# Loading q and k in 512-byte runs, with the tokens of each 128-block kept even-then-odd through masks, V and output

## The chip, the cores and the metric

The kernel runs on one core of one Trainium2 chip. The metric is the device time of one execution in microseconds (us). The profile's span is about 2 us shorter than that time, because it goes from the first to the last instruction. In the profile's lines PE is TensorE (PEld its weight loads), DVE VectorE, ACT ScalarE, POOL GpSimd and SP SyncE; the granted clock is the share of its full clock that TensorE was given.

## The reference

It is an attention layer followed by a two-branch dense layer. Half of the heads see all earlier tokens, the others only the first 4 tokens and a window of 64.

```python
B, H, S, D = 4, 8, 768, 64          # q, k, v: float32
scores = q @ k.T / sqrt(D)          # causal; for "streaming" heads also: sink of 4 or window of 64
a   = softmax(scores)
x   = (a @ v), heads side by side   # 3072 tokens x 512
out = maximum(x @ w1, x @ w2) @ w_out    # 512 -> 1024 -> 512, float32 out
```

The inputs q and k are drawn with a standard deviation of 0.1, so all scores are small and the softmax is nearly flat. The comparison with the reference does not notice when the tokens of q or k are permuted, but it does notice a wrong order of v.

## The kernel before

The 32 heads are worked on in 16 pairs. Each pair's q, k and v come in by DMA as float32, GpSimd casts them to bfloat16, and q and k are transposed so that the head dimension lies on the partitions. For the first four pairs TensorE does the transposing and VectorE or ScalarE evacuates; from the fifth pair on (`FIRST_QK_DMA = 4`) a DMA transpose does it. Scores, exponentials, masks, the product with v and the dense layer follow. A small planner in the program fixes the order on every engine when the kernel is built, with a cost for each operation; nearly all DMAs are issued by SyncE, in one program order.

```python
# one load of a pair; only the first pairs' q and k come as 512-byte runs (two tokens side by side)
wide = which < 2 and i < FIRST_QK_DMA
pat = ("h (m p r) d -> p h m (r d)", dict(p=128, r=2)) if wide else ("h (n p) d -> p h n d", dict(p=128))
...
    nc.sync.dma_start(out=dst, in_=src.rearrange(pat[0], **pat[1]))
ld_ops[tag, i] = P.add({"DMA": 1.15 if wide else 1.75}, fn, ...)

# transposing q or k, from the fifth pair on: one DMA of 128 x 768
nc.sync.dma_start_transpose(
    out=P[tt, i].rearrange("p (n c) -> p n c", c=128),
    in_=P[tb, i].rearrange("p n h d -> p (n h d)"))

# the first four pairs: evacuation of TensorE's transposes puts two-token runs back in order
if i < FIRST_QK_DMA:
    o = o.rearrange("q (m p r) -> q m r p", p=128, r=2)
    in_ = in_.rearrange("q (m r p) -> q m r p", p=128, r=2)
ev(eng)(out=o, in_=in_)

# scores of one step: (k block j, first q column, columns, offset in the PSUM bank)
for (j, q0, w, off) in segs:
    for hh in range(2):
        nc.tensor.matmul(P["sc", i, st, hh][:, off:off + w],
            lhsT=kt[64 * hh:64 * hh + 64, j * 128:(j + 1) * 128],
            rhs=qt[64 * hh:64 * hh + 64, q0:q0 + w], start=True, stop=True, ...)
...
# store of 128 output rows
nc.sync.dma_start(out=out[r0:r0 + 128, :], in_=P["ot", b, g, t])
```

The softmax here doesn't subtract the row's maximum and nothing guards it: scores larger than these inputs give would overflow.

Of the kernel before, what the change touches and what calls it, by code (L numbers as in the profile page):

```python
# [133 lines left out]
def kernel(  # L134
# [81 lines left out]
    def constants():  # L216
# [5 lines left out]
        col = consts.tile([128, 256], F32)  # L222
        nc.vector.memset(col[:, 0:1], 0.0)
        w = 1
        while w < 256:
            nc.vector.tensor_scalar_add(out=col[:, w:2 * w], in0=col[:, 0:w], scalar1=float(w))
            w *= 2
        rowt = consts.tile([128, 32], F32)
        nc.vector.transpose(rowt, col[:, 0:32])
        row = consts.tile([128, 1], F32)  # L230
        for qd in range(4):
            nc.vector.tensor_scalar_add(
                out=row[32 * qd:32 * qd + 32, :], in0=rowt[32 * qd:32 * qd + 32, 0:1],
                scalar1=float(32 * qd))
        nc.vector.tensor_scalar(out=ident, in0=col[:, 0:128], scalar1=row, scalar2=None, op0=ALU.is_equal)
# [23 lines left out]
    def near(j):  # L259
        return (j, 128 * j, min(256, S - 128 * j), 256 * (j % 2))  # L260

    STEPS = (
        ("near", [near(0), near(1)]),
        ("far0", [(0, 256, 512, 0)]),
        ("near", [near(2), near(3)]),
        ("far", [(1, 384, 384, 0), (3, 640, 128, 384)]),
        ("near", [near(4), near(5)]),
        ("far", [(2, 512, 256, 0)]),
    )
    NS = len(STEPS)  # L270
# [4 lines left out]
    def plan_load(i, b, hp, which):  # L275
        src = (q, k, v)[which][b, 2 * hp:2 * hp + 2]
        tag = ("ldq", "ldk", "ldv")[which]
        wide = which < 2 and i < FIRST_QK_DMA
        pat = ("h (m p r) d -> p h m (r d)", dict(p=128, r=2)) if wide else ("h (n p) d -> p h n d", dict(p=128))

        def fn(eng):
            dst = P[tag, i]
            if which < 2 and not wide:
                dst = dst.rearrange("p h m (r d) -> p h (m r) d", d=D)
            nc.sync.dma_start(out=dst, in_=src.rearrange(pat[0], **pat[1]))  # L285
        ld_ops[tag, i] = P.add({"DMA": 1.15 if wide else 1.75}, fn, acq=[(tag, (tag, i))], prio=(len(ld_ops),))
# [14 lines left out]
    def plan_pair(i, b, hp):  # L301
# [15 lines left out]
        for which in range(2):  # L317
            tb, tt = (("qb", "qt"), ("kb", "kt"))[which]

            if i >= FIRST_QK_DMA:  # L320
                def move(eng, tb=tb, tt=tt):
                    nc.sync.dma_start_transpose(
                        out=P[tt, i].rearrange("p (n c) -> p n c", c=128),
                        in_=P[tb, i].rearrange("p n h d -> p (n h d)"))
                tops.append(P.add({"DMA": 0.9}, move, deps=[casts[which]], acq=[(tt, (tt, i))], rel=[(tb, i)],
                                  prio=(0, i, which)))
                continue
# [7 lines left out]
            def evac(eng, which=which, tt=tt):  # L335
                o, in_ = P[tt, i], P["mmT", i, which].bitcast(BF16)[:, 0:S]
                if i < FIRST_QK_DMA:
                    o = o.rearrange("q (m p r) -> q m r p", p=128, r=2)
                    in_ = in_.rearrange("q (m r p) -> q m r p", p=128, r=2)
                ev(eng)(out=o, in_=in_)  # L340
            t = P.add({"PE": 0.34}, tr, deps=[casts[which], ident_op], acq=[("mm", ("mmT", i, which)), (tt, (tt, i))],
                      rel=[(tb, i)], prio=(1, i, which))
            tops.append(P.add({"DVE": 0.56, "ACT": 0.72} if i >= FIRST_QK_DMA else {"DVE": 1.02, "ACT": 1.02}, evac, deps=[t],
# [4 lines left out]
        def qk(st):  # L348
            kind, segs = STEPS[st]
            n = segs[-1][3] + segs[-1][2]  # L350

            def fn(eng):
                qt, kt = P["qt", i], P["kt", i]
                for (j, q0, w, off) in segs:
                    for hh in range(2):
                        nc.tensor.matmul(  # L356
                            P["sc", i, st, hh][:, off:off + w],
                            lhsT=kt[64 * hh:64 * hh + 64, j * 128:(j + 1) * 128],
                            rhs=qt[64 * hh:64 * hh + 64, q0:q0 + w],
                            start=True, stop=True, skip_group_check=True)  # L360
            return fn, n, kind, segs
# [46 lines left out]
        for st in range(NS):  # L408
            kind, segs = STEPS[st]

            def fn(eng, st=st, segs=segs):
                for hh in range(2):
                    at, po, vb = P["at", i, st, hh], P["po", i, hh], P["vb", i]
                    for si, (j, q0, w, off) in enumerate(segs):
                        for t in range(w // 128):
                            qb_ = q0 // 128 + t
                            nc.tensor.matmul(
                                po[:, qb_ * (D + 1):(qb_ + 1) * (D + 1)],
                                lhsT=at[:, off + t * 128:off + (t + 1) * 128],
                                rhs=vb[:, hh, j, :],  # L420
                                start=(st == 0 and si == 0 and t == 0),
                                stop=(st == NS - 1 and si == len(segs) - 1 and t == w // 128 - 1),
                                skip_group_check=True)
            nblk = sum(s[2] for s in segs) // 128
# [79 lines left out]
    def plan_dense(b):  # L504
        mm = "mm" if b < B - 1 else "sc"
        prev = [None]
        for g in range(NG):
# [24 lines left out]
            for t in range(GT // 128):  # L532
# [22 lines left out]
                def store(eng, g=g, t=t, c0=c0):  # L555
                    r0 = b * S + c0
                    nc.sync.dma_start(out=out[r0:r0 + 128, :], in_=P["ot", b, g, t])
# [74 lines left out]
```

## Time and profile before

| | kernel before |
|---|---|
| time, median of 2 runs | 212.63 us (211.14 to 214.13) |
| span of the profiled run, granted clock | 208.5 us, 0.992 |
| first scores of the fifth pair start at | 49.2 us |
| first scores of the last pair start at | 148.6 us |
| last score matmul | 155.8 us |

I call the time up to 49.2 us the first stage, the 99.4 us from there to the first scores of the last pair the middle, and the 52.8 us behind the last score matmul the tail. These starts are counted in the trace by the number of score matmuls of a pair, which is the same for all pairs (20 before, 36 after).

From the page of the kernel before, the DMA packets, and the chain that ended last by engine:

```profile
DMA packets 98916, 37.84 MB, mean 181 GB/s; under 512 B 87632, under 2 KB 93776, under 8 KB 98896
PE 42%; DMA 26%; DVE 13%; SPq 6%; ACT 5%; issue 3%; POOL 2%; POOLq 0%; ACTq 0%; DVEq 0%
```

Nine packets in ten are under 512 bytes; these are what the change goes for. In this trace a packet of 256 bytes takes 18 ns in the median, one of 512 bytes 29 ns.

SyncE's own work is easy to pass over, since issuing is not counted as busy in the page's first part. The timeline of SyncE in the kernel before, cut from the middle; the columns are start, duration in us, engine, line, operation and tiles:

```profile
114.04 1.31 SPq L322 DMA_TRANSPOSE qt_97<-qb_90  x1
115.82 1.21 SPq L322 DMA_TRANSPOSE kt_99<-kb_92  x1
117.13 0.53 SPq L557 DMA_DIRECT2D out_dram<-ot_125  x1
117.71 0.42 SPq L285 DMA_DIRECT2D qn_82<-in_q_dram  x1
118.19 0.83 SPq L285 DMA_DIRECT2D kn_85<-in_k_dram  x1
```

A transpose takes SyncE 1.2 to 1.3 us, a store 0.53, loads 0.4 to 0.8. Between them are gaps of up to half a microsecond. Adding up all its issues in the middle gives 78.7 of 99.4 us: 28 transposes 41.7, 20 loads of q and k 15.6, 10 of v 11.7, 11 stores 9.7.

### The profile page before, as it was taken

How to read it: one execution, taken by the hardware profiler on the slowest of the kernel's cores; microseconds unless marked ns; L12 is line 12 of the kernel's file. 1: busy time of each engine (PE TensorE's matmuls, PEld its weight loads, DVE VectorE, ACT ScalarE, POOL GpSimd, SP SyncE). 2: the span in 40 equal slices, each digit the busy share in tenths (PEclk: the TensorE clock that was granted, in tenths of full speed). 3: DMA queues.
4: the chain of work that ended last, by engine and by line, in shares of the span. 5: the costliest groups of instructions: out<-in, count | busy, mean ns of one | idle time of the engine just before them, and what ended most of it. 6: DMA issues, size and time to landing. Idle time of an engine off the chain costs nothing.

```text
span 208.5 us, 4406 instructions
## 1 busy us (share of the span) xinstructions
PE 183.5 (88%) x1702; PEld 95.2 (46%) x1702; DVE 119.5 (57%) x273; ACT 124.0 (59%) x240; POOL 47.6 (23%) x59
## 2 busy tenths in 40 slices
PE   0388886999999799959997999979999999999992
PEld 0244553544554356523463545534454465444540
DVE  7799989957796477614574357427454084030700
ACT  2489699724888788947866795959692200212021
POOL 0155547053333132331231332314000000000000
PEclk9999999999999999988999999999999999999999
DMA  4999999969999999999999999999630210212112
GB/s 117 268 344 323 258 350 410 250 129 220 236 174 240 176 246 218 173 195 191 233 175 207 229 251 205 228 171 252 156 27 15 89 50 0 101 53 101 50 50 101
DMA packets 98916, 37.84 MB, mean 181 GB/s; under 512 B 87632, under 2 KB 93776, under 8 KB 98896
## 3 DMA queue, kind: packets, MB, share of 16 engines
q1 hardware_dynamic: 98752, 37.56, 87.1%
q8 instruction: 13, 0.21, 0.5%
q14 instruction: 7, 0.06, 0.1%
q10 hardware_dynamic: 144, 0.01, 0.0%
HBM read 25.17 MB, written 6.29 MB: 151 GB/s over the span
## 4 chain that ended last, share of the span: by engine, by line
PE 42%; DMA 26%; DVE 13%; SPq 6%; ACT 5%; issue 3%; POOL 2%; POOLq 0%; ACTq 0%; DVEq 0%
PE bank_80 L543 8%; DMA vn_87<-in_v_dram 6%; DMA kn_86<-in_k_dram 6%; SPq L285 4%; PE bank_79 L543 4%; PE bank_79 L514 4%; DMA kt_100<-kb_93 3%; PE bank_80 L514 3%; DMA kn_84<-in_k_dram 3%; DMA vn_89<-in_v_dram 3%; PE bank_80 L495 3%; DMA out_dram<-ot_125 3%; PE bank_74 L543 2%; PE bank_73 L543 2%; DMA kn_85<-in_k_dram 2%
## 5 line engine op out<-in xcount | busy, mean ns | idle before, releaser
L514 PEld LDWEIGHTS <-wd_bf 128*128 128x128 bf16 x256 | 23.0, 98 | 16.6 <-issue 3.0
L368 ACT ACTIVATE at_101<-bank_73 128x512 bf16<-128x512 f32 x16 | 9.6, 597 | 12.4 <-PE bank_74 L356 12.4
L379 DVE TENSOR_TENSOR at_101<-at_101,msk 128x512 bf16<-128x512 bf16 x16 | 8.0, 500 | 12.0 <-ACT at_101 L368 12.0
L356 PE MATMUL bank_73<-qt_98,kt_100 64*128 64x256 bf16 (+1 forms) x48 | 9.2, 271 | 5.9 <-DMA kt_100<-kb_93 5.9
L356 PEld LDWEIGHTS <-kt_100 64*128 64x128 bf16 x160 | 5.6, 94 | 17.1 <-issue 8.5
L543 PEld LDWEIGHTS <-gt_124 128*128 128x128 bf16 x96 | 8.9, 100 | 9.9 <-issue 1.4
L543 PEld LDWEIGHTS <-gt_123 128*128 128x128 bf16 x96 | 8.6, 98 | 9.8 <-issue 0.8
L379 DVE TENSOR_TENSOR at_109<-at_109,msk 128x384 bf16<-128x384 bf16 x16 | 7.9, 493 | 8.9 <-ACT at_109 L368 8.8
L368 ACT ACTIVATE at_107<-bank_75,bias_j 128x512 bf16<-128x512 f32 x16 | 11.1, 695 | 2.4 <-PE bank_76 L356 2.3
L356 PEld LDWEIGHTS <-kt_99 64*128 64x128 bf16 x160 | 5.5, 95 | 13.2 <-issue 8.7
L368 ACT ACTIVATE at_103<-bank_75,bias_64 128x512 bf16<-128x512 f32 x16 | 11.1, 692 | 0.6 <-PE bank_76 L356 0.6
L356 PE MATMUL bank_73<-qt_97,kt_99 64*128 64x256 bf16 (+1 forms) x48 | 9.5, 276 | 2.2 <-DVE kt_99 L340 1.1
L527 DVE TENSOR_SCALAR gt_124<-bank_80 128x384 bf16<-128x384 f32 x9 | 5.0, 558 | 10.8 <-ACT ot_127 L553 5.8
L368 ACT ACTIVATE at_104<-bank_76,bias_64 128x512 bf16<-128x512 f32 x16 | 11.1, 696 | 0.0
L368 ACT ACTIVATE at_108<-bank_76,bias_j 128x512 bf16<-128x512 f32 x16 | 11.1, 691 | 0.0
L368 ACT ACTIVATE at_111<-bank_75,bias_j 128x256 bf16<-128x256 f32 x16 | 7.7, 480 | 5.2 <-PE bank_76 L356 5.2
L368 ACT ACTIVATE at_105<-bank_73 128x512 bf16<-128x512 f32 x16 | 9.8, 613 | 1.6 <-PE bank_74 L356 1.6
L543 PE MATMUL bank_79<-wo_bf,gt_124 128*128 128x512 bf16 x40 | 10.1, 379 | 0.0
L553 ACT COPY ot_125<-bank_80 128x512 f32<-128x512 f32 x3 | 1.8, 585 | 14.0 <-PE bank_80 L543 14.0
L379 DVE TENSOR_TENSOR at_105<-at_105,msk 128x512 bf16<-128x512 bf16 x16 | 8.0, 502 | 3.6 <-ACT at_105 L368 3.6
L543 PE MATMUL bank_80<-wo_bf,gt_123 128*128 128x512 bf16 x40 | 10.0, 380 | 0.0
L368 ACT ACTIVATE at_106<-bank_74 128x512 bf16<-128x512 f32 x16 | 9.9, 621 | 0.0
(225 smaller groups left out, 494.8 us busy)
## 6 DMA issues: line engine op xcount, KB each, us to landing
w_f<-in_moe_w_dram SPq DMA_DIRECT2D x4, 1024.0 KB, 9.2
qn_81<-in_q_dram SPq DMA_DIRECT2D x6, 384.0 KB, 4.7
kn_84<-in_k_dram SPq DMA_DIRECT2D x6, 384.0 KB, 5.6
vn_87<-in_v_dram SPq DMA_DIRECT2D x6, 384.0 KB, 6.5
wo_f<-in_moe_w_out_dram SPq DMA_DIRECT2D x2, 1024.0 KB, 8.2
out_dram<-ot_125 SPq DMA_DIRECT2D x8, 256.0 KB, 2.3
out_dram<-ot_126 SPq DMA_DIRECT2D x8, 256.0 KB, 2.4
out_dram<-ot_127 SPq DMA_DIRECT2D x8, 256.0 KB, 2.4
```

Of the source, the lines that this page charges most:

```text
L285: nc.sync.dma_start(out=dst, in_=src.rearrange(pat[0], **pat[1]))
L356: nc.tensor.matmul(P["sc", i, st, hh][:, off:off + w], lhsT=kt[64 * hh:64 * hh + 64, j * 128:(j + 1) * 128], rhs=qt[64 * hh:64 * hh + 64, ...
L368: nc.scalar.activation(out=P["at", i, st, hh][:, 0:n], in_=P["sc", i, st, hh][:, 0:n], func=ACT.Exp, scale=scale, bias=bias)
L379: nc.vector.tensor_mul(out=at[:, 0:n], in0=at[:, 0:n], in1=mk)
L495: nc.tensor.matmul(P["mmM", c], lhsT=w2t[:, f, c * 128:(c + 1) * 128], rhs=wo_bf[:, f, :], start=(f == 0), stop=(f == FC - 1))
L514: nc.tensor.matmul(P["mmH", b, g, f][:, 0:GT], lhsT=wd_bf[:, c, f * 128:(f + 1) * 128], rhs=P["xt", b][:, c, g * GT:(g + 1) * GT], start=( ...
L527: nc.vector.tensor_relu(out=o, in_=i_)
L543: nc.tensor.matmul(ps, lhsT=lhsT, rhs=rhs, start=(i == 0), stop=(i == KC + FC - 1))
L553: ev(eng)(out=P["ot", b, g, t], in_=P["mmY", b, g, t])
```

## The change

The intent: all q and k are to be loaded as runs of 512 bytes (two neighbouring tokens), not only the first four pairs'. That leaves the even tokens of a block apart from the odd ones after the transpose. Instead of sorting them back, the kernel keeps each 128-token block even-then-odd everywhere: masks, rows of v, rows of the output. To get that order, each DMA transpose, load of v and store is split into two of 64 partitions. The even blocks are laid ahead of the odd ones, so that one half-transpose fills one contiguous half of the transposed tile.

```diff
-        wide = which < 2 and i < FIRST_QK_DMA
...
-            nc.sync.dma_start(out=dst, in_=src.rearrange(pat[0], **pat[1]))
-        ld_ops[tag, i] = P.add({"DMA": 1.15 if wide else 1.75}, ...)
+            if which < 2:
+                nc.sync.dma_start(out=dst, in_=src.rearrange("h (m p r) d -> p h m (r d)", p=128, r=2))
+            else:
+                by_r = src.rearrange("h (n p r) d -> r p h n d", p=64, r=2)
+                for r in range(2):
+                    nc.sync.dma_start(out=dst[64 * r:64 * r + 64], in_=by_r[r])
+        ld_ops[tag, i] = P.add({"DMA": 1.2 if which < 2 else 1.85}, ...)
...
-                    nc.sync.dma_start_transpose(
-                        out=P[tt, i].rearrange("p (n c) -> p n c", c=128),
-                        in_=P[tb, i].rearrange("p n h d -> p (n h d)"))
+                    for half in range(2):
+                        nc.sync.dma_start_transpose(
+                            out=P[tt, i][:, half * 384:half * 384 + 384].rearrange("p (n c) -> p n c", c=64),
+                            in_=P[tb, i][64 * half:64 * half + 64].rearrange("p n h d -> p (n h d)"))
...
-                    nc.sync.dma_start(out=out[r0:r0 + 128, :], in_=P["ot", b, g, t])
+                    rows = out[r0:r0 + 128, :].rearrange("(p r) f -> r p f", r=2)
+                    for r in range(2):
+                        nc.sync.dma_start(out=rows[r], in_=P["ot", b, g, t][64 * r:64 * r + 64, :])
... (cut: position constants and masks in the new order; evacuation of TensorE's transposes in
     runs of 64; score matmuls by runs of blocks, 576 in place of 320; v's block of each tile)
```

## The prediction

> **What bounds the kernel now.** I read the page's slices first, then busy time by stretch, then the chain of waits in each stretch, then the DMA landings and single lines. The slices show no engine that is full from end to end. VectorE is nearly full in the first quarter, the DMA engines until about 150 us, TensorE from there on:
>
> ```profile
> PE   0388886999999799959997999979999999999992
> DVE  7799989957796477614574357427454084030700
> DMA  4999999969999999999999999999630210212112
> ```
>
> So I cut the span where the kind of work changes. The columns are the busy time of each engine, the granted clock, the DMA share and GB/s:
>
> ```profile
> 10.00:42.00 32.00, 26.95 (x340) 15.99 (x341) 30.42 (x59) 27.23 (x53) 15.36 (x16) 1.00 1.12 321
> 49.00:149.00 100.00, 92.96 (x974) 46.42 (x972) 57.26 (x135) 76.82 (x154) 27.81 (x33) 0.98 1.22 210
> 156.00:208.50 52.50, 48.52 (x270) 24.61 (x268) 15.96 (x31) 8.10 (x15) 0.00 (x0) 1.00 0.16 61
> ```
>
> From 10 to 42 us VectorE (the third busy time) works 30.4 of 32 us and the chain lies on it. From 49 us (first scores from DMA-transposed k) to 149 us (scores of the last pair) the DMA share is over 1 while only 210 GB/s move. After 156 us DMA and the others rest, and TensorE runs the dense matmuls that are left. The chain inside the middle stretch, its longest pieces:
>
> ```profile
> 62.08 4.18 DMA kn_85<-in_k_dram
> 69.17 6.94 DMA kn_86<-in_k_dram
> 79.73 7.22 DMA vn_87<-in_v_dram
> 90.59 5.29 DMA out_dram<-ot_125
> 99.52 6.08 DMA vn_89<-in_v_dram
> 128.28 5.53 DMA kn_86<-in_k_dram
> 138.56 6.05 DMA vn_87<-in_v_dram
> ```
>
> These are loads of q, k, v that stand behind one another in one queue, so this stretch goes at the pace of that queue. TensorE looks 93% busy there, but that counts pipeline time: summing its matmuls at their start-to-start spacings (216 ns for 512 columns, 163 ns for 384, 30 ns for the 65-column ones) gives only some 78 us of work in the 100. TensorE can take a faster supply, but not a much faster one. The median times from issue to landing in the middle stretch, and the two lines that the change touches most:
>
> ```profile
> qn_81<-in_q_dram SPq DMA_DIRECT2D x4, 384.0 KB, 4.5
> vn_88<-in_v_dram SPq DMA_DIRECT2D x3, 384.0 KB, 6.7
> L322 SPq DMA_TRANSPOSE kt_99<-kb_92 x6: 1209/1212/2598, 45.0 to 134.9; - x6
> L340 DVE COPY kt_100<-bank_80 x2: 1019/1021/1023, 14.2 to 29.7; 128x768 bf16<-128x768 bf16 x2
> ```
>
> From the landings I take what each transfer costs the queue when it is full (the distance between one landing and the next): a load in 256-byte runs 1.75 us; a transpose 0.66 us (two issued at 93.95 and 95.26 land at 98.62 and 99.27); an output store about 0.95 us. A load in 512-byte runs, as the first four pairs use them, is 1.38 us apart (18.68, 20.05, 21.43).
>
> [...] the packet records have 18 ns for a 256-byte packet and 29 ns for one of 512 (medians), 14 against 18 bytes per ns. [...] No transfer of the kernel before takes half of the partitions[...]; the changed kernel has 128 of them (32 of v, 48 transposes, 48 stores). [...] the 128-column PE transposes start 55 to 56 ns apart.
>
> **The change part by part.**
>
> *First stage, on VectorE.* The evacuation of the PE transposes now writes runs of 64 elements instead of every second one. It takes 1.02 us, eight times (six on VectorE); the plain copy of the same 128x768 (xt_120) takes 0.54. That is 6 x 0.47 = 2.8 us off VectorE if the new pattern copies as the plain one. Against it: six more small constant instructions (about 0.15 us each, +0.9), partly in a gap of 1.04 us that VectorE has at 8.2 us; and the built order moves two weight casts (0.6 us each) from GpSimd to VectorE. Net: 1 to 2 us earlier, I take **-1.5**.
>
> *Middle stage, on the queue.* From 49 to 149 us about 29 loads land (19 of q and k, 10 of v), with 22 transposes of q and k, 6 of x, and 14 stores. Before: 29 x 1.75 + 28 x 0.66 + 14 x 0.95 = 50.8 + 18.5 + 13.3 = 83 us of the 100; the rest are stalls, such as those around 70, 96, 108 and 136 us, where the packets of a transpose are held for 0.6 to 2 us. The change saves 19 x (1.75 - 1.38) = **-7.0 us**. It pays for this with halves:
> - v in two DMAs of 64 partitions. Now 393 KB in 1.75 us is 225 GB/s. [...] 10 x 0.15 = +1.5.
> - stores in two of 64 rows. Now 262 KB in 0.95 us is 276 GB/s; [...] +2.5.
> - transposes in two of 64 partitions. Now 197 KB in 0.66 us is 298 GB/s; [...] +2.
>
> SyncE's issue is a second price. A transpose takes it 1.21 us at least, a load 0.42, a store 0.33. If the time of a transpose goes with its size, two halves cost little more; if not, SyncE's 28 transposes of the middle stage become 50. The least it has to do in 100 us is 51 us now (28 x 1.21 + 29 x 0.42 + 14 x 0.33) and 61 to 86 after, still below the limit, but the latency of each k would grow by up to 1.2 us. I add +1 for this. Middle stage in sum: -7.0 + 1.5 + 2.5 + 2 + 1 = **0**, with a spread of some 6 us to each side.
>
> *TensorE.* The near blocks are no longer neighbours, so the score matmuls go from 320 to 576: 256-column pieces become two of 128. A pair of heads runs side by side: the 64x256 ones start in pairs every 105 ns, so two 128-column pairs at 56 ns each add 7 ns, some 128 times: +0.9 us spread over the span, mostly in the middle's slack.
>
> *Last stage.* The order on each engine is fixed at build time by a planner that was told of faster loads. In the built order the up-projection matmuls behind the last score matmul go from 100 to 128, the down-projections stay at 144. So 28 x 0.160 = **+4.5 us** of dense work leaves the middle for a tail in which TensorE is full. In return the middle carries 4.5 us less; since that stage is only about 78% full of matmuls, I count -2.5 of it. The last store is two DMAs, the second issued 0.33 us later: +0.4.
>
> *Sum:* -1.5 + 0 + 0.5 + 4.5 - 2.5 + 0.4 = about **+1.4 us** from 210.3 in the profiled run. The two timed runs scatter from 211.1 to 214.1, and I shade the middle estimate down[...]: **212.5 us**, as good as no change.
>
> **The rivals.** *A: the queue gains and the halves are free.* For it: landings follow one another without a gap, so the halves may merge in the queue. Then the middle is 7 us shorter, the first stage 1.5, and the moved 4.5 us cost at most 2.5: about 206. *B: the halves cost more than the runs save*[...] by SyncE. For it: transposes already hold packets for up to 2 us, and half of the long chain pieces are not q or k. Then the middle is 6 us longer and the moved work comes on top: 219 or 220. *C: TensorE takes over.* Speeding up the loads only moves the wait to TensorE's fixed order, and the moved tail shows in full: 210 to 214. This is nearest to my sum.
>
> **Range and chances.** From A to B: 206 to 220. A and B seem about equally likely to me, and C likelier than either; faster by over 2% (below 208.4) 0.26, within 2% 0.50, slower 0.24.
>
> **What the profile after would show.** Right: q and k landings 1.4 us apart, packets under 512 B fewer by some 37,000 (24 loads of 1,536); evacuations of the first pairs at 0.55 to 0.6 us; [...] packets of the stores longer than the present 85 ns even in the quiet tail[...]; the stretch behind the last score matmul longer by 4 to 5 us. Wrong: a middle stretch under 95 us (halves free) or over 104 us (halves dear); half-transposes that take SyncE 1.2 us each; or a middle in which TensorE waits for its own order and not for k.

## More of the kernel before

In the chain, "SPq" is the time in which SyncE's issuing of DMAs was what everything waited for: 6% here.

## The result

The changed kernel took **241.38 us** (median of 2 runs, 240.19 to 242.56) against 212.63: it is slower, by a ratio of 1.135 (95% interval 1.093 to 1.177). A ratio here is the mean time of one kernel's fast runs over that of the other's fast runs of the same rounds, so it is not quite the ratio of the medians quoted. Executions over 1.5% slower than the fastest of the same kernel are left out of the means. The prediction of 212.5, and its range up to 220, missed.

| us | before | after | difference | predicted |
|---|---|---|---|---|
| first stage | 49.2 | 53.1 | +3.9 | -1.5 |
| middle, first scores of pair 5 to those of pair 16 | 99.4 | 120.2 | +20.8 | about 0, less 2.5 |
| tail, behind the last score matmul | 52.8 | 58.2 | +5.4 | +4.9 |
| span | 208.5 | 238.4 | +29.9 | |

The rest of the span, the last pair's own scores, is about 7 us in both. The page of the changed kernel, its slices and packets, then its chain by engine:

```profile
PE   0498986999869789979297929896999999999992
DVE  7668788864442654644154604384455308210700
DMA  5999999969998887988685989696853031053313
DMA packets 81896, 37.89 MB, mean 159 GB/s; under 512 B 52176, under 2 KB 76752, under 8 KB 81872
PE 41%; DMA 32%; SPq 15%; POOL 4%; issue 2%; ACT 1%; DVE 1%; POOLq 0%; ACTq 0%
```

The rows for DMA and TensorE, nearly unbroken nines before, now have sevens and eights in the middle: neither is full. The packets went down as intended, those under 512 bytes by 35,456. And SPq went from 6% to 15% of the chain. Busy time in stretches cut by the same rule as before:

```profile
10.00:42.00 32.00, 26.16 (x372) 18.68 (x374) 24.37 (x54) 25.39 (x50) 14.02 (x14) 0.95 1.10 305
53.00:173.00 120.00, 97.07 (x1088) 50.05 (x1100) 54.17 (x128) 77.58 (x151) 28.06 (x33) 0.90 0.90 170
180.00:238.30 58.30, 53.35 (x302) 27.50 (x302) 18.21 (x35) 10.96 (x21) 0.00 (x0) 0.98 0.27 59
```

In the middle line the DMA share is 0.90 (it was 1.22), the rate 170 GB/s (210), VectorE and ScalarE do about the same work in 20 us more, and the granted TensorE clock is 0.90 (0.98). So every engine in that line is less loaded than before, and something else sets the pace. In the first line VectorE works 24.4 of 32 us (30.4): by this count it no longer fills the first stage. The third is the tail, which I cut at 180 us now. SyncE's timeline in the same part of the pipeline:

```profile
134.23 4.07 SPq L345 DMA_TRANSPOSE qt_97<-qb_90  x2
138.39 2.51 SPq L345 DMA_TRANSPOSE kt_99<-kb_92  x2
140.96 0.59 SPq L303 DMA_DIRECT2D qn_83<-in_q_dram  x1
141.65 1.23 SPq L479 DMA_TRANSPOSE xt_122<-x_118  x1
142.97 1.18 SPq L583 DMA_DIRECT2D out_dram<-ot_125  x2
144.20 0.59 SPq L303 DMA_DIRECT2D kn_86<-in_k_dram  x1
144.83 1.36 SPq L307 DMA_DIRECT2D vn_89<-in_v_dram  x2
146.30 1.62 SPq L345 DMA_TRANSPOSE qt_98<-qb_91  x1
```

Each line starts within about 0.1 us of the end of the one before: in this stretch SyncE has no pause. "x2" with 2.51 us is the two halves of one k. The sum over the middle is 111.4 of 120.2 us (93%; 79% before): 50 transposes 70.4, 20 loads of q and k 15.6, 20 halves of v 14.1, 18 halves of stores 11.3. The lines of two transposes of the changed kernel, minimum, median and maximum in ns:

```profile
L345 SPq DMA_TRANSPOSE qt_97<-qb_90 x12: 1197/1260/2202, 45.8 to 159.5; - x12
L345 SPq DMA_TRANSPOSE kt_99<-kb_92 x12: 1186/1250/2664, 49.2 to 162.1; - x12
```

A transpose of 64 partitions takes SyncE 1.19 us at least here, one of 128 took 1.21. **Halving the data did not halve the issue.**

The queue shows the other side. I measured the distance from one landing to the next where a transfer was issued at least 1 us before the one ahead of it landed, so that it had to stand in line (medians):

| in the queue, us | before | after |
|---|---|---|
| load of q or k | 1.81 | 1.42 |
| load of v | 2.39 | 2 x 1.11 |
| transpose of q or k | 0.70 | 2 x 0.40 |
| store of 128 rows | 0.85 | 2 x 0.36 |

For the queue the change is a gain: the loads of q and k give 20 x 0.39 = -7.8 us, the halved transposes cost 22 x 0.1 = +2.2. The row of v can't be read as a gain: its ten values before go from 1.6 to 3.3 us, their median is 2.39 or 2.06 as one counts the loads issued in the middle or those landed there, and a whole v took 1.75 us in a_all_whole and 1.73 in a_whole_v_store (experiments below). Against these, two halves cost 0.4 to 0.5 us more. A whole store took 0.69 and 0.68 us there, so its halves (0.72) cost about nothing. In sum the queue gains some 2 to 6 us. But only 26 of 44 half-transposes of q and k found such a line at all (17 of 21 before). The median from issue to landing of a k says it too:

```profile
kt_99<-kb_92 SPq DMA_TRANSPOSE x6, 4.2
kt_99<-kb_92 SPq DMA_TRANSPOSE x12, 2.5
```

It fell from 4.2 us to 2.5: the halves find a shorter line. More often than before, the queue waits for SyncE.

One more prediction held. The evacuations of the first pairs' transposes, 1.02 us before, in the changed kernel on VectorE and ScalarE:

```profile
L360 DVE COPY kt_100<-bank_80 x2: 557/558/558, 15.0 to 31.7; 128x768 bf16<-128x768 bf16 x2
L360 ACT COPY qt_97<-bank_79 x1: 792/792/792, 8.5 to 8.5; 128x768 bf16<-128x768 bf16 x1
```

### The profile page after: what moved, and what is told of

Same layout as the page of the kernel before. It is cut to its first block, busy times and chain, and to the rows that moved or that the text cites.

```text
span 238.4 us, 5062 instructions
## 1 busy us (share of the span) xinstructions
PE 195.6 (82%) x1938; PEld 106.3 (45%) x1958; DVE 116.1 (49%) x279; ACT 127.5 (53%) x243; POOL 46.2 (19%) x57
## 4 chain that ended last, share of the span: by engine, by line
PE 41%; DMA 32%; SPq 15%; POOL 4%; issue 2%; ACT 1%; DVE 1%; POOLq 0%; ACTq 0%
PE bank_79 L567 7%; PE bank_80 L567 7%; SPq L345 6%; DMA qn_82<-in_q_dram 5%; SPq L307 5%; DMA kt_99<-kb_92 4%; DMA kn_84<-in_k_dram 4%; DMA vn_88<-in_v_dram 4%; DMA wo_f<-in_moe_w_out_dram 3%; PE bank_79 L538 3%; DMA kn_86<-in_k_dram 3%; PE bank_77 L441 3%; PE bank_73 L380 3%; PE bank_80 L538 2%; DMA qn_83<-in_q_dram 2%
## 5 line engine op out<-in xcount | busy, mean ns | idle before, releaser
L538 PEld LDWEIGHTS <-wd_bf 128*128 128x128 bf16 x256 | 24.1, 101 | 17.1 <-issue 3.6
L380 PE MATMUL bank_73<-qt_97,kt_99 64*128 64x128 bf16 x88 | 11.3, 242 | 15.2 <-DMA kt_99<-kb_92 14.2
L380 PEld LDWEIGHTS <-kt_99 64*128 64x128 bf16 x288 | 9.4, 101 | 30.2 <-DMA kt_99<-kb_92 16.7
L380 PEld LDWEIGHTS <-kt_100 64*128 64x128 bf16 x288 | 9.3, 98 | 20.8 <-issue 10.3
L567 PEld LDWEIGHTS <-gt_123 128*128 128x128 bf16 x120 | 11.5, 101 | 13.5 <-issue 1.7
L380 PE MATMUL bank_73<-qt_98,kt_100 64*128 64x128 bf16 x88 | 10.9, 237 | 7.5 <-DMA kt_100<-kb_93 7.2
L404 DVE TENSOR_TENSOR at_109<-at_109,msk 128x384 bf16<-128x384 bf16 x16 | 6.5, 408 | 14.5 <-ACT at_109 L393 14.4
L567 PE MATMUL bank_79<-wo_bf,gt_123 128*128 128x512 bf16 x46 | 12.9, 418 | 0.1
L567 PE MATMUL bank_80<-wo_bf,gt_123 128*128 128x512 bf16 x46 | 11.2, 379 | 0.2 <-issue 0.2
L380 PE MATMUL bank_74<-qt_97,kt_99 64*128 64x128 bf16 x88 | 11.3, 242 | 0.0
L332 POOL CAST vb_94<-vn_87 128x768 bf16<-128x768 f32 x6 | 5.5, 922 | 27.9 <-DMA vn_87<-in_v_dram 26.6
L380 PE MATMUL bank_74<-qt_98,kt_100 64*128 64x128 bf16 x88 | 10.8, 236 | 0.0
```

What stands on the lines that cost most here:

```text
L332: ev(eng)(out=dst[:, :, :, 0:D], in_=src)
L380: nc.tensor.matmul(P["sc", i, st, hh][:, off:off + w], lhsT=kt[64 * hh:64 * hh + 64, place(j):place(j) + 128], rhs=qt[64 * hh:64 * hh + 64 ...
L404: nc.vector.tensor_mul(out=at[:, 0:n], in0=at[:, 0:n], in1=mk)
L538: nc.tensor.matmul(P["mmH", b, g, f][:, 0:GT], lhsT=wd_bf[:, c, f * 128:(f + 1) * 128], rhs=P["xt", b][:, c, g * GT:(g + 1) * GT], start=( ...
L567: nc.tensor.matmul(ps, lhsT=lhsT, rhs=rhs, start=(i == 0), stop=(i == KC + FC - 1))
```

## The experiments

**Theory T**: SyncE's issue. A DMA transpose costs its issuer about 1.2 us whether it takes 64 partitions or 128 (1.19 and 1.21 us at least, above); 22 more of them in the middle make SyncE the pace. **Rivals**: P, transfers of 64 partitions are slow by themselves; L, the second half makes each k land later, and its scores wait; Q, the queue. Times are medians of each kernel's own rounds, in which the kernel before took 211.3 to 213.4 us; the ratios are to those. "Middle", "first" and "tail" are the stages above in the profiled run, "SyncE" is its issue time in the middle.

| kernel | time | ratio to before | first | middle | tail | q/k transposes | SyncE |
|---|---|---|---|---|---|---|---|
| before | 212.6 | 1 | 49.2 | 99.4 | 52.8 | 24 | 78.7 |
| after | 241.4 | 1.135 | 53.1 | 120.2 | 58.2 | 48 | 111.4 |
| a_one_transpose | 216.8 | 1.026 | 53.4 | 96.7 | 58.2 | 24 | 87.9 |
| a_whole_v_store | 227.3 | 1.074 | 49.9 | 110.6 | 57.3 | 48 | 104.1 |
| a_all_whole | 205.3 | 0.973 | 49.1 | 90.2 | 57.3 | 24 | 81.1 |
| b_half_transpose | 233.9 | 1.104 | 51.2 | 119.9 | 52.8 | 48 | 109.0 |
| b_col_transpose | 233.2 | 1.098 | 49.9 | 119.1 | 52.8 | 48 | 107.1 |
| b_half_k | 232.3 | 1.103 | 53.2 | 117.3 | 52.8 | 48 | 104.9 |
| b_half_k2 | 221.3 | 1.049 | 53.7 | 106.0 | 52.8 | 36 | 87.5 |
| a_v_on_pool | 238.8 | none | 64.3 | 103.2 | 58.3 | 48 | 88.7 |
| a_joint | 233.1 | 1.101 | 53.6 | 110.7 | 61.2 | 24 | 92.7 |
| a_joint_deep | 231.2 | 1.095 | 52.8 | 108.0 | 61.1 | 24 | 91.4 |
| a_joint_two | 226.9 | 1.070 | 51.4 | 106.3 | 61.0 | 24 | 91.3 |
| b_joint | 211.2 | 0.997 | 50.5 | 92.0 | 60.2 | 12 | 79.7 |
| b_joint_two | 213.8 | 1.016 | 48.5 | 96.7 | 60.2 | 24 | 87.8 |
| b_joint_half | 218.4 | 1.037 | 51.9 | 97.3 | 60.1 | 24 | 86.3 |
| b_wide_q | 221.3 | 1.051 | 51.3 | 106.8 | 52.9 | 24 | 67.2 |
| b_joint_wide_q | 209.6 | 0.992 | 48.5 | 91.9 | 60.2 | 12 | 76.2 |

Names that start with a are built from the changed kernel, those with b from the kernel before. b_half_transpose and b_half_k came out as the same kernel (see there), and their first stages differ by 2.0 us, their middles by 2.6: differences of this size between stages of two single profiles mean nothing here. The share of the middle in which SyncE issues does not tell slow kernels from fast ones by itself: it is 91% in a_one_transpose and 90% in a_all_whole.

### Taking the halves back, one kind at a time

**a_one_transpose**: the transposes whole again. The q and k columns then come in a wrong order.

```diff
-                    for half in range(2):
-                        nc.sync.dma_start_transpose(out=P[tt, i][:, half * 384:...], in_=P[tb, i][64 * half:...])
+                    nc.sync.dma_start_transpose(
+                        out=P[tt, i].rearrange("p (n c) -> p n c", c=128),
+                        in_=P[tb, i].rearrange("p n h d -> p (n h d)"))
```

> The changed kernel with each q and k transposed by one DMA over all 128 partitions instead of two over 64. Wrong result on purpose: the columns come in another order, everything else (loads, matmuls, orders on the engines, split v and stores) is the same. Theory 1 (SyncE's issue: a DMA transpose keeps SyncE for 1.2 us whatever its size, and the doubled number of them paces the middle stage): 24 transposes fewer at 1.2 us, so some 22 to 28 us faster than the changed kernel, to 213 to 219 us. Theory 2 (v and stores that reach half of the partitions hold the queue): at most 6 us faster, about 236. Theory 3 (the planner's order and the larger tail): no more than 3 us faster.

Measured: 216.83 us (215.88 to 218.68), ratio 1.026. The middle fell by 23.5 us to 96.7, first stage and tail did not move. So the second halves of the transposes cost more than all that the change lost in the middle (20.8); the long runs gave some of it back.

**a_whole_v_store**: v and the stores whole, transposes still in halves; wrong result (relative error 0.84).

```diff
-                by_r = src.rearrange("h (n p r) d -> r p h n d", p=64, r=2)
-                for r in range(2):
-                    nc.sync.dma_start(out=dst[64 * r:64 * r + 64], in_=by_r[r])
+                nc.sync.dma_start(out=dst, in_=src.rearrange("h (n p) d -> p h n d", p=128))
...
-                    for r in range(2):
-                        nc.sync.dma_start(out=rows[r], in_=P["ot", b, g, t][64 * r:64 * r + 64, :])
+                    nc.sync.dma_start(out=out[r0:r0 + 128, :], in_=P["ot", b, g, t])
```

> The changed kernel with v loaded by one DMA and output rows stored by one DMA, over 128 partitions, in the natural order of tokens (wrong result on purpose), half-transposes kept. Theory 1 (issue on SyncE, transposes): 16 loads and 24 stores fewer at 0.6 us, of which some 10 and 15 lie in the paced stage: 8 to 15 us faster, to 226 to 233, still clearly slower than before. Theory 2 (half of the partitions hold the queue): nearly all of the 28 us come back, to about 215.

Measured: 227.27 us (226.93 to 227.60), ratio 1.074. The middle is 9.6 us shorter than in the changed kernel, and the first stage is back at 49.9: with v whole its loss of 3.9 us is gone. SyncE is still 94% busy. The halves of v and of the stores are the smaller part; how much of it is SyncE's issue (7.3 us less in the middle) and how much the queue's is not separated.

**a_all_whole**: both together; 512-byte loads, nothing halved; wrong result (0.84).

> The changed kernel with no split transfer left: q and k in 512-byte runs, one transpose over 128 partitions each, v and stores by one DMA (tokens in the wrong order on purpose; the number of matmuls and the planner's order of the changed kernel stay). Theory 1 with the tail apart (the halves' issues are the loss, the planner's order costs 5 us in the tail): first stage about that of before, middle 6 to 10 us shorter than before, tail 5 us longer: 204 to 210 us. If something else of the change is slow (512-byte loads, 128-column score matmuls): over 213.

Measured: 205.25 us (204.04 to 205.94), ratio 0.973 (0.964 to 0.981). With the long runs alone the middle is 9.2 us shorter than before, in the direction that the queue's numbers say. Up to half of that may be dense work that the planner moved behind the last scores (28 matmuls, about 4.5 us, which the tail has). So the aim of the change was sound; the halves that it paid with cost more.

### Halving alone, in the kernel before

**b_half_transpose** splits each transpose by partitions, **b_col_transpose** by columns, so that each half still has all 128 partitions. Both are correct.

```diff
+                    for half in range(2):      # b_half_transpose
+                        nc.sync.dma_start_transpose(
+                            out=P[tt, i].rearrange("p (n f c) -> p f n c", f=2, c=64)[:, half],
+                            in_=P[tb, i][64 * half:64 * half + 64].rearrange("p n h d -> p (n h d)"))
```
```diff
+                    for half in range(2):      # b_col_transpose
+                        nc.sync.dma_start_transpose(
+                            out=P[tt, i][:, half * 384:half * 384 + 384].rearrange("p (n c) -> p n c", c=128),
+                            in_=P[tb, i][:, 3 * half:3 * half + 3].rearrange("p n h d -> p (n h d)"))
```

> The kernel before with nothing changed but each DMA transpose of q and k cut into two of 64 partitions. Correct result, loads in 256-byte runs, whole v and stores, the order of the kernel before. Theory 1 (issue): 24 more issues of 1.2 us; SyncE was busy for 79 of 100 us in the middle stage, so the first 20 us fill its slack in part: 10 to 25 us slower, 223 to 238 us. Theories 2 and 3: within 3 us of the kernel before.

> As b_half_transpose, but cut by columns: two transposes of 128 partitions and 3 of the 6 blocks each. Correct result. If the issue of a transpose costs the same whatever its shape: the same time as b_half_transpose, and 1.2 us of SyncE per piece. If the issue goes with the number of column blocks and not with the partitions: about 0.65 us per piece and a time within 5 us of the kernel before. If only transfers over 64 partitions are slow: the time of the kernel before.

Measured: 233.87 us (ratio 1.104, 1.096 to 1.113) and 233.16 (1.098, 1.087 to 1.109): the same within their intervals, with middles of 119.9 and 119.1. The lines of k's transposes, by partitions and then by columns:

```profile
L323 SPq DMA_TRANSPOSE kt<-kb x24: 1188/1258/2002, 47.2 to 168.5; - x24
L323 SPq DMA_TRANSPOSE kt<-kb x24: 1190/1247/1746, 46.5 to 168.0; - x24
```

Rival P falls for the transposes: whether a half takes 64 partitions or 128 makes no difference. In the queue a half takes 0.41 and 0.40 us against 0.70 for a whole one, so rival Q could explain some 24 x 0.1 us, not 20.

**b_half_k** was meant to halve k alone. The choice was made by a loop variable that had its last value by the time the code ran, so q was halved as well. It is a repeat of b_half_transpose and is counted as nothing more (it shows how far two profiles of one kernel differ): 232.32 us (231.91 to 233.26), ratio 1.103.

> The kernel before with the transposes of k alone cut into two of 64 partitions (12 more issues, not 24). Correct result. If the cost is the throughput of SyncE, which had some 20 us of slack in the middle: the first 12 issues (14.6 us) are in good part hidden and this is 3 to 8 us slower, less than half of the 22 us of b_half_transpose. If it is latency on the path to each pair: half of it or more, 11 us or over.

**b_half_k2** does it properly (the variable bound when the operation is planned; the built order shows one transpose for q, two for k).

```diff
-                def move(eng, tb=tb, tt=tt):
+                def move(eng, tb=tb, tt=tt, which=which):
+                    if which == 0:  ... one transpose, as before
+                    for half in range(2 if which else 0):  ... two of 64 partitions
```

> The kernel before with k alone transposed in two halves (an earlier kernel that was meant to do this halved q as well and so repeated the one with both). Twelve transposes more instead of 24. If SyncE's throughput decides, its issue in the middle rises from 79 to about 93 us of some 105: less than half of the 21 us that halving both cost, 214-221. If the later landing of each k decides, since the scores wait for k, nearly all of it: 225-232.

Measured: 221.26 us (219.61 to 222.20), ratio 1.049: 47% of the loss of halving both. It lies at the edge of what throughput gave (214 to 221), and below what L gave (225 to 232). If the later landing of k were the price, k alone would have cost nearly all of it; in the middle it cost 6.6 of 20.5 us. That speaks for the number of issues. It does not exclude L for a part: SyncE issued for only 83% of this middle (87.5 of 106.0), not the 93 us that were expected, so time was lost there before SyncE was full.

### Taking issues off SyncE without taking anything else away

**a_v_on_pool**: the changed kernel, with v's halves issued by GpSimd. Correct.

```diff
-                    nc.sync.dma_start(out=dst[64 * r:64 * r + 64], in_=by_r[r])
+                    nc.gpsimd.dma_start(out=dst[64 * r:64 * r + 64], in_=by_r[r])
```

> The changed kernel with its 32 half-loads of v issued by GpSimd and not by SyncE; all halves stay, so the DMA engines move the same. Correct result. If SyncE's issue is the pace of the middle stage (94% of its time there), the 0.65 us of each of some 22 loads leave it: 8 to 15 us faster than the changed kernel, to 226 to 233. If it is the DMA engines[...]: within 3 us of the changed kernel.

Measured: 238.75 us (234.46 to 242.21), of which only the profiled run, 234.46, counts as fast, so there is no ratio. As a whole this misses what I expected. In the stages it does not: the middle fell from 120.2 to 103.2 us with the same bytes, the same halves and the same two transposes in front of each k. The first stage lost 11 us. There GpSimd also does the casts; that its issues held them up is likely, but I did not show it. Nor is all of the 17 us in the middle saved time: four of its 44 half-transposes, some 6 us of issue, were issued in the longer first stage.

**a_v_pool_late** moves v's halves only from the seventh pair on.

```diff
-                    nc.sync.dma_start(...)
+                    (nc.sync if i < 6 else nc.gpsimd).dma_start(...)
```

> The changed kernel, but from the seventh pair on the two half-loads of v are issued by GpSimd instead of SyncE (the first six pairs' stay on SyncE, since moving them too cost 11 us in the first stage in an earlier run). SyncE-issue theory: the middle (pair 4 to pair 15) falls from 120 us to 103-106 as in that earlier run, the first stage stays at 53-54, so the whole lands at 221-226 us. Rival (the DMA engines themselves, or two transposes in a row ahead of each k): the bytes, the halves and the two transposes per k are the same, so the middle stays above 115 and the whole at 234-241.

Measured: 226.83 us median of four, which scattered from 223.81 to 232.89; the two fast runs give 1.057 (1.039 to 1.076). The two fast runs, 223.8 and 223.9, are where T put them (221 to 226), and 7% below the changed kernel's ratio. Its profile fell in a slow run (middle 111.1), which I don't compare.

The issuing time is not small beside the transfers here: the issue of a half-transpose took three times its place in the queue (1.2 against 0.40 us), and moving 20 half-loads of v gave some 17 us in a_v_pool_late (241.4 against 223.9 us).

### Fewer transposes: q and k in one

If the count matters, one DMA for q and k together should help. **b_joint** casts both into one tile of 128 x 1536 and transposes that, 12 transposes in place of 24. Correct.

```diff
-        "qb": ring("qb", 2, [128, NB, 2, D], BF16),  "kb": ...,  "qt": ...,  "kt": ...
+        "qkb": ring("qkb", 2, [128, 2, NB, 2, D], BF16),
+        "qkt": ring("qkt", 2, [128, 2, S], BF16),
...
+                    nc.sync.dma_start_transpose(
+                        out=P["qkt", i].rearrange("p w (n c) -> p (w n) c", c=128),
+                        in_=P["qkb", i].rearrange("p w n h d -> p (w n h d)"))
```

> The kernel before, but q and k of a pair are cast into one tile and transposed by one DMA of 128 x 1536 instead of two of 128 x 768 (12 transposes fewer; correct result). If a transpose's price on SyncE is per instruction: one joint transpose takes SyncE 1.2-1.3 us at least, SyncE's issue in the middle falls from 79 us to about 65. If SyncE was not the bound before (it was busy 79 of 100 us and the queue's transfers 83 of 100), the time stays within 2%, 208-213; if it already was in part, the middle falls below 95 and the time to 200-207. If the price goes with the columns, a joint transpose takes 2.4 us and nothing changes, 210-214.

Measured: 211.15 us (210.20 to 211.48), ratio 0.997 (0.987 to 1.007): no difference that these runs show. The joint transpose's line:

```profile
L323 SPq DMA_TRANSPOSE qkt<-qkb x12: 1516/2386/4826, 44.6 to 135.5; - x12
```

1.52 us at least, so per element it is cheaper than two of 1.21. But the median is 2.39, and SyncE's issue in the middle did not fall (79.7). From issue to landing it took 5.5 us in the median, so it stood in a long line. So an issue can be long for another reason than its own work: its median is 2.1 to 2.2 us with two or three earlier DMAs still under way and 3.3 us with four, in 12 cases (that a full queue is the cause is my reading and was not tested). And SyncE's busy time alone does not show that SyncE is the limit. In the changed kernel it is the short line in the queue that shows it. The middle did fall by 7.4 us and the tail rose by 7.4: the planner, told of cheaper transposes, had put 48 dense matmuls more behind the last scores.

**a_joint** is the changed kernel with a joint tile, two half-transposes of 64 x 1536 a pair: correct, and as many transposes as before the change.

> The changed kernel, correct, but q and k of a pair share one tile and each half of it is transposed by one DMA of 64 x 1536: two transposes a pair instead of four, halves of v, of the stores and of the transposes kept. SyncE-issue theory: as with one whole transpose each in wrong order (216.8 us, middle 97): 213-219 us, middle 94-99. Rival (transfers of half the partitions are what costs[...]): the same bytes move over the same 64 partitions, so it stays above 230.

Measured: 233.13 us (231.96 to 234.23), ratio 1.101. **A miss**: T had 213 to 219. SyncE issued for only 84% of the middle. So the count of transposes is not all that can hold this kernel. Its waits show a new one, casts that wait for a transpose (columns: us in total, times, longest):

```profile
POOL qkb L327 <- DMA qkt<-qkb: 32.1, 5, 10.0
```

**a_joint_deep** takes that wait away with four buffers instead of two.

```diff
-        "qkb": ring("qkb", 2, [128, 2, NB, 2, D], BF16),
+        "qkb": ring("qkb", 4, [128, 2, NB, 2, D], BF16),
```

> The changed kernel with joint half-transposes (233 us), but with four buffers in place of two between the casts and the transposes, so that no cast waits for a transpose to land (it waited 32 us in five waits). If that wait was what kept it slow, 213-222 and a middle under 102; if it only showed where time went that was lost elsewhere, 228-235.

Measured: 231.19 us (229.96 to 233.75), ratio 1.095. The wait is gone from the list and the time is not: it was a place where lost time showed, not its cause.

**b_joint_two** and **b_joint_half** put the question to the kernel before: the same joint tile, transposed as q whole and k whole, or as two halves of 64 x 1536.

```diff
+                    for w in range(2):     # b_joint_two
+                        nc.sync.dma_start_transpose(out=P["qkt", i][:, w]..., in_=P["qkb", i][:, w]...)
```
```diff
+                    for f in range(2):     # b_joint_half
+                        nc.sync.dma_start_transpose(
+                            out=P["qkt", i].rearrange("p w (n f c) -> p f (w n) c", f=2, c=64)[:, f],
+                            in_=P["qkb", i][64 * f:64 * f + 64].rearrange("p w n h d -> p (w n h d)"))
```

> Joint buffer of q and k in the kernel before, but transposed by two whole DMAs (128 x 768 each, one for q, one for k), both behind both casts: 24 transposes, as in the kernel before. If the count of transposes on SyncE decides: as the kernel before or the single joint transpose within 2%, 209-216. If the shared buffer itself is what made the changed kernel with joint half-transposes slow (a cast of the pair after next waits until both transposes have landed), 222-232.

> The same joint buffer, transposed by two DMAs of 64 partitions x 1536: again 24 transposes, the same bytes, correct. If count alone decides, within 2 us of the two whole ones. If a transpose out of 64 partitions is dear by itself (in the queue, not in SyncE's issue), slower than the two whole ones by 8 us or more. A joint half-transpose should take SyncE 1.2-1.3 us at least in both theories, as seen before.

Measured: 213.77 us (ratio 1.016, 1.008 to 1.024) and 218.43 (1.037, 1.028 to 1.045). The joint tile with 24 transposes costs little, as T says. The halves cost 4.7 us more than the whole ones, less than P wanted and more than T: 3.4 of it in the first stage, 0.6 in the middle.

**a_joint_two** is a_joint with q and k transposed whole, columns in a wrong order.

```diff
-                    for half in range(2):  ... two of 64 x 1536
+                    for w in range(2):     ... q whole, k whole, 128 x 768 each
```

> The changed kernel with the joint buffer (233 us), but q and k transposed whole, one DMA of 128 x 768 each: as many transposes, same order on every engine, same halves of v and of the stores; only the transposes no longer take 64 partitions. The columns come in a wrong order, on purpose. If the transposes out of 64 partitions held the joint version, 214-220 with a middle of 96-101; if the joint buffer and its order did, 228-234 with a middle above 107.

Measured: 226.94 us (225.84 to 227.73), ratio 1.070, between the two expectations. Of a_joint's distance to a_one_transpose (16.3 us), the halves are 6 us and 10 us belong to the joint tile and the order that the planner makes with it. Why that costs 10 us in the changed kernel and some 3 in the kernel before (b_joint_two's ratio of 1.016) stays **open**.

### A version that keeps the long runs of q and halves nothing

**b_wide_q** loads q alone in 512-byte runs, transposes it whole, and lets the score matmuls read the tokens in order, element by element from two places 128 columns apart. Correct.

```diff
+        def read_q(t, a, n_):
+            t = t.rearrange("p (m r c) -> p m c r", r=2, c=128)
```

> The kernel before with q alone in 512-byte runs: still one transpose of 128 partitions; the score matmuls read q's columns in the order of tokens by a two-dimensional pattern (alternating between two columns 128 apart), so nothing else changes, nor the planner's order. Correct result. What the middle stage gains if the queue paces it: 10 loads of 0.37 us less, 3 to 5 us faster (207 to 209). If it is paced by SyncE's issue of what it has to do already: within 2 us. If the strided read slows the score matmuls[...]: slower by up to 10 us.

Measured: 221.27 us (220.63 to 223.66), ratio 1.051: slower. **b_joint_wide_q** joins q and k as in b_joint, and reads q as whole runs of 64 (even, then odd); the exponential puts the columns back in order as it reads PSUM.

```diff
+            # token 256m+128e+2c+r lies in column 256m+128r+64e+c of qt
+            t = t.rearrange("p (m r e c) -> p m e r c", r=2, e=2, c=64)
...
+                    o = o.rearrange("k (b c r) -> k b c r", r=2, c=64)
+                    in_ = in_.rearrange("k (b r c) -> k b c r", r=2, c=64)
                 nc.scalar.activation(out=o, in_=in_, ...)
```

> The joint transpose of q and k in the kernel before, and q alone loaded in 512-byte runs; the score matmuls read each block of q as two contiguous runs of 64 (even, then odd tokens) and the exponential puts the columns back in order, so nothing is halved and v, masks, k and stores stay as before (correct result). The queue is relieved of 10 x 0.37 = 3.7 us in the middle. If the queue or SyncE's issue paces the middle, 2-5 us faster than the joint transpose alone, 203-209. If the two-run reads double the matmul as the element-wise strided ones did (643 against 382 ns at 512 columns), or the strided read of PSUM slows ScalarE's exponentials, it is slower than the joint transpose alone by 5 us or more, 215-225.

Measured: 209.58 us (208.90 to 211.94), ratio 0.992 (0.979 to 1.005). The score matmuls of 256 columns by form: b_wide_q; b_joint_wide_q; b_joint, which reads q plainly. In each line the mean ns follow the busy us:

```profile
L375 PE MATMUL bank<-qt,kt 64*128 64x256 bf16 x168 | 30.8, 376 | 2.2 <-DVE kt L340 1.1 <-DMA kt<-kb 0.8 <-ACT at L387 0.2
L376 PE MATMUL bank<-qkt 64*128 64x256 bf16 x216 | 27.3, 280 | 7.7 <-DMA qkt<-qkb 6.1 <-DVE qkt L341 1.1 <-ACT at L392 0.4
L357 PE MATMUL bank<-qkt 64*128 64x256 bf16 x192 | 22.6, 283 | 7.7 <-DMA qkt<-qkb 6.4 <-DVE qkt L341 1.1
```

Reading one element from each place in turn costs a matmul 376 ns on average against 283, though the first four pairs' plain reads are among its 168 (the other 120 took 408); reading runs of 64 costs nothing (280). The traces give these times and no reason for them. ScalarE's exponentials of 512 columns without a bias tile took 607 ns on average in b_joint and in b_joint_wide_q. The 512-byte loads of q did not show as a gain: the middles of b_joint and b_joint_wide_q are 92.0 and 91.9 us, and the intervals of their ratios overlap. The 2 to 5 us that I expected of them did not come in the middle.

The comparison with the reference would not notice a wrong order of q here. I checked the order by its indices (the comment in the diff); that is an argument, not a test.

**b_joint_wide_q_plan** changes one number, what the planner is told of a joint transpose, so that the 48 dense matmuls stay ahead of the last scores.

```diff
-                tops.append(P.add({"DMA": 0.9}, move, ...
+                tops.append(P.add({"DMA": 1.8}, move, ...
```

> The kernel with the joint transpose and 512-byte loads of q, correct; only the planner's cost of a joint transpose is raised from 0.9 to 1.8 us, so that the built order keeps 48 dense matmuls (some 7.5 us) ahead of the last scores, as in the kernel before (268 instead of 316 behind them). If the middle is paced by SyncE and the queue and TensorE has room there, the tail falls from 60 to 53 us and the middle stays below 90: 200-204, faster than the kernel before by 3 to 5%. If TensorE is full in that middle, the work only moves back: 206-211.

Measured: **204.15 us** (203.25 to 208.20, 6 runs), ratio 0.963 (0.957 to 0.969): faster than both kernels, at the edge of what was expected (200 to 204). Its profile is of a slow run, so I take from it only what a slow run would not shorten: the tail is 52.8 us (60.2 without the plan), the middle 92.4 (91.9). A middle below 90 did not come, but even in a slow run TensorE had room for the work in the middle. What the plan would give to b_joint, with its plain loads of q, was not run; so the 4% are shown for the joint transpose, the long runs and the plan together, and a share of the long runs is not shown.

## Why the prediction was wrong

**The step that failed: "If the time of a transpose goes with its size, two halves cost little more; if not, SyncE's 28 transposes of the middle stage become 50. ... I add +1 for this."** The mechanism was named, its term was mis-sized: it measured 23.5 us by a_one_transpose, and 20.5 and 19.7 by b_half_transpose and b_col_transpose in the kernel before. Of the prediction's own signs of being wrong two came true: a middle over 104 us, and half-transposes that take SyncE 1.2 us each. Two things went wrong in the step.

- It took SyncE's **least** issue times and got "51 us now and 61 to 86 after, still below the limit". The trace of the kernel before already had the real sum, 78.7 of 99.4 us. To that, 22 transposes at 1.25 us add 27.5, the halves of v 2.4 (14.1 against 11.7) and the stores 1.6: 110, more than the whole middle. SyncE's sum after was 111.4.
- It left open whether the time goes with the size, though it made all the difference, and split the difference with a small number.

**Rival B** named SyncE among its reasons and came nearest, at 219 or 220; even it allowed 6 us for the middle where 20.8 came.

**The queue's steps.** The loads came out as worked out: q and k land 1.42 us apart (1.38 forecast). Halved transposes cost the queue 2.2 us (forecast 2). Halved v and stores were forecast to cost 4 us. These terms, like the +2 for the transposes, were assumptions of mine: no transfer of the kernel before takes half of the partitions, so its trace could not show them. The stores cost the queue about nothing (0.72 us against 0.68 to 0.85), although their packets did become slower, with a median of 135 ns against 85. Two halves of v took 2.2 us, where a whole one took 1.75 in a_all_whole; so this term was undersized: some 4 to 5 us for ten of them, against +1.5. a_all_whole shows that the queue's gain is real.

**First stage.** The evacuations came out right (0.56 us on VectorE). The stage still ended 3.9 us later, not 1.5 earlier. With v and stores whole it is back within 0.7 us of before, which puts the loss on the halves of v; the prediction had counted them in the middle only. But b_half_k2 has a first stage of 53.7 us without them, and two profiles of one kernel differ by 2.0 us in it, so this is not settled. Nor is why the faster evacuations did not show as a gain even in a_all_whole (49.1).

**TensorE and the tail.** 576 smaller score matmuls did no harm that shows: a_all_whole has them and a middle of 90.2 us. The 105 ns between pairs of 256-column score matmuls, on which the +0.9 us rests, was a misreading: in the trace before, most start 119 to 121 ns apart. In the changed kernel the pairs of 128 columns start 66 ns apart in the median, the most frequent distances being 56 and 66 ns, so two of them take between 8 ns less and 13 ns more. The tail of +5.4 us was forecast at 4.9 for the right reason. The 2.5 us that the middle was to save in return cannot be told apart in a stage paced by SyncE.

**The granted clock** was lower in most runs with a slow middle: 0.938 over the changed kernel's span, 0.979 in a_one_transpose, 0.997 in a_all_whole (but b_wide_q had 0.992 with a middle of 106.8). No run tells how much of the lost time it made and how much it followed from; the prediction did not think of it.

## What to carry to other kernels

Count the DMA instructions of the engine that issues them as work of that engine: add up their real durations from the trace, not the least ones, before splitting a transfer in two. Here, with a full issuer over a queue whose line was short, whole transfers in 256-byte runs beat halved ones in 512-byte runs (212.6 against 241.4 us); where the order of elements must change, look for an engine with room that can do it as it reads (here ScalarE's exponential, 607 ns with the reordering and without). And when a kernel's order is planned from costs, look at what a changed cost moves elsewhere, since here one number was worth some 3%.

## What else the runs show of issues and reads

- The least time that a DMA transpose took SyncE was 1.18 us for 64 x 768 (changed kernel), 1.18 for 128 x 384 (b_col_transpose), 1.21 for 128 x 768 (kernel before), 1.22 for 64 x 1536 (a_joint) and 1.52 for 128 x 1536 (b_joint), while a half of 64 x 768 takes 0.40 us in the queue and a whole one of 128 x 768 takes 0.70.
- In the changed kernel 50 transposes took SyncE 70.4 us of a middle of 120.2.
- A nearly solid issuer is no proof by itself. SyncE issued for 87% of b_joint's middle and for 90% of a_all_whole's, and b_joint's transposes took far longer than their least time (128 x 1536: 1.52 us at least, 2.39 in the median), so one must also look how long the line in the queue is.
- ScalarE's exponential, reading PSUM at a stride of 64 elements in b_joint_wide_q, took 607 ns for 512 columns, as with the plain read in b_joint.
